# Three jobs of weight sums in the first pair of the second MLP instead of two, and another order of its SBUF pools

## The chip, the cores and the metric

One NeuronCore of a Trainium2 chip runs the whole program. The metric is the device time of one execution in microseconds; lower is better.

## The reference

Attention with sparse masks feeds two MLPs, all in float32:

```python
x = attention(q, k, v)            # 2304 tokens x 512; q, k, v: 4 x 8 heads x 576 x 64
h = np.maximum(x @ w_in, 0.0)     # w_in 512 x 2048
x = (s * h * h + b) @ w_out       # w_out 2048 x 512
a = x @ w_a                       # w_a, w_b 512 x 1536
b2 = x @ w_b
out = (a * b2) @ w_out2           # w_out2 1536 x 512
```

## The kernel before, in words

TensorE multiplies in float32r, each factor split into a high and a low part, three products for one. The first MLP runs in blocks of tokens (`n`), and in each over 16 columns of weights (`f`): `h_mm`, then `o_mm` two steps later. The last block is `n == NB - 1`. Its accumulators leave for `o1s` tiles, which are stored to DRAM for the second MLP.

The second MLP uses a Strassen-like form: every 2 by 2 block product needs seven products, and four sums of the weights' quarters (`s1` to `s4`). One call of the generator `sums(g, ...)` is one **job**: it loads two tiles `w2r` from DRAM on POOL's queue, makes the four sums in a tile `w2t` on DVE, copies highs on ACT into a room, subtracts lows on DVE, and stores the lot to DRAM on POOL's queue. Jobs 0 to 11 belong to w_a and w_b (two stores of 512 KB, `w2s`), jobs 12 to 17 to w_out2 (four stores, 1,792 KB together, `w2o`). A job of the second kind takes 14 steps of the generator: the loads, four sums, four copies, four subtractions, the stores and the end.

Sixteen jobs run in the last block of the first MLP, one called at each `f` by `work(f)`, in the order 0 to 3, 12 to 15, 4 to 11. Their highs lie, from the fourth job on, in one tile `room` of the pool `xp1` (`spare_s`, two places used in turn; `spare_a` beside it serves the jobs of w_out2 alone). Jobs 16 and 17 run in the first pair of the second MLP, spread over its groups one step at a time by `job_at` and `job_step`; their highs lie in buffers of the ring of g forms (`gf`).

The second MLP goes over three pairs of token blocks; in each, 12 groups `g` make seven products of six matmuls each (`a11`, `s2`, `s3`, `s1`, `a12`, `a22`, `s4`, in that order on TensorE) and gather them in `quad` tiles (one of pool `gq` for two groups); the last matmuls (`o2_mm`) follow. A group's weights come by `fill` and `source` on SP's queue: `wf` straight from `w2s`, and `wsrc`, which ACT and DVE split into `wf` and `wh`. Two helpers, `act` and `dve`, keep ACT's and DVE's instructions of this part in the order of the program.

In group 0 the first product is copied by ACT into the first quad (`u = qd[:, 1]`). The fifth product (`a12`) goes to the same PSUM bank, so it waits for that copy.

The pools that close with the first MLP (`mlp1.close()`) are, in KB of a partition: `xp0` 0 to 16, `xp1` 16 to 30, `wpb` 30 to 78 (counted from the first of them). The second MLP's pools lie over them in the order of their opening: `ws` 4, `tmp` 9, `rp` 15, `gq` 36, `rq` 12, `wx` 2, and each new tile waits for every use of each old tile that it lies over, as a whole (`reuse_waits="tile"`). So in the kernel before `gq` begins at 28 KB; its first tile, 28 to 34 KB, lies over the last 2 KB of `room`, where `spare_a` ends, and over `wpb`.

Of the kernel before, what the change touches and what calls it, by code (L numbers as in the profile page):

```python
# [27 lines left out]
def sparse_attention_two_mlps(  # L28
# [22 lines left out]
    NF1 = FF1 // P  # L51
# [52 lines left out]
    @contextmanager  # L104
    def after(instructions):
        with ExitStack() as st:
            for i in instructions:
                st.enter_context(tc.issue_after(i))
            yield

    def in_order(step, *args):
        with after(list(last_pe)):
            return step(*args)
# [7 lines left out]
    def split(hi, lo, src):  # L121
        nc.scalar.activation(out=hi, in_=src, func=AF.Copy)  # L122
        return nc.vector.tensor_tensor(out=lo, in0=src, in1=hi.bitcast(F32), op=ALU.subtract)
# [726 lines left out]
    p2 = None  # L850
    NG2 = NF2
    NQ2 = NF2 // 2
    EARLY = NF1

    def sums(g, room, vector, scalar):
        own = g < NG2
        first_ = 6 * (g // 2) + g % 2 if own else 6 * (g - NG2) + 2
        r = [p2.tile([P, DM], F32, tag="r", name="w2r", bufs=4) for _ in range(2)]
        for t, i in zip(r, (first_, first_ + 3)):
            nc.gpsimd.dma_start(out=t, in_=w2d[i])  # L860
        yield
        quarter = lambda t, i: t[:, i * HALF:(i + 1) * HALF]
        a11, a22 = quarter(r[0], 0), quarter(r[1], 1)
        a12, a21 = (quarter(r[0], 1), quarter(r[1], 0)) if own else (quarter(r[1], 0), quarter(r[0], 1))
        t = p2.tile([P, 4, HALF], F32, tag="s", name="w2t", bufs=2)
        s2, s1, s3, s4 = (t[:, i] for i in range(4))
        for out_, in0, in1, op in (
            (s1, a21, a22, ALU.add), (s2, s1, a11, ALU.subtract),
            (s3, a11, a21, ALU.subtract), (s4, a12, s2, ALU.subtract),
        ):  # L870
            vector(out=out_, in0=in0, in1=in1, op=op)  # L871
            yield
        flat = lambda t: t.rearrange("p i c -> p (i c)")
        zs, zh, zl = room(g)
        n = 4 * HALF // len(zs)
        halves_ = [(flat(t)[:, i * n:(i + 1) * n], z) for i, z in enumerate(zs)]
        lows = [i.bitcast(F32R) for i, _ in halves_]
        if not own:
            halves_ += [(r[1], zh[:, HALF:]), (a11, zh[:, 0:HALF])]
            lows += [zl[:, HALF:], zl[:, 0:HALF]]  # L880
        for src, high in halves_:
            scalar(out=high, in_=src, func=AF.Copy)  # L882
            yield
        for (src, high), low in zip(halves_, lows):
            vector(out=low, in0=src, in1=high.bitcast(F32), op=ALU.subtract)
            yield
        m = (2 if own else 4) // len(zs)
        for e in range(2):
            for i, z in enumerate((zs, lows)[e][:len(zs)]):
                nc.gpsimd.dma_start(  # L890
                    out=w2s[g][:, :, e] if own else w2o[g - NG2][:, 3 + i * m:3 + (i + 1) * m, e],
                    in_=z.bitcast(F32).rearrange("p (i c) -> p i c", i=m),
                )
            if not own:
                nc.gpsimd.dma_start(
                    out=w2o[g - NG2][:, 0:3, e], in_=(zh, zl)[e].bitcast(F32).rearrange("p (i c) -> p i c", i=3)
                )
        yield
# [36 lines left out]
    def x2_load(pair):  # L935
        xr = p2.tile([P, 2, KD, TB2], F32, tag="xr", name="xr")
        for i in range(2):
            c0 = (2 * pair + i) * TB2
            queue_sp(out=xr[:, i], in_=o1[:, c0:c0 + TB2].rearrange("(k p) t -> p k t", p=P))
        return xr  # L940
# [164 lines left out]
    for n in range(NB):  # L1105
        acc = [ps_acc.tile([P, TM], F32, tag="acc", name="acc") for _ in range(KD)]
        if n == 1:
            with after(list(behind)):
                split(bc[:, 0], bc[:, 1], b_sb.to_broadcast([P, 2]))
        if n + 1 == NB:  # L1110
            assert not steps
            att.close()
            p2 = ctx.enter_context(tc.tile_pool(name="p2", bufs=1, reuse_waits="tile", side="right"))
            spares = cycle(range(2))
            rooms_s = lambda g: (
                [spare if len(begun) < 4 else spare_s[next(spares)]], *(spare_a if g >= NG2 else 2 * [None])
            )
            first_jobs = [*range(0, 4), *range(NG2, NG2 + NQ2 - 2), *range(4, NG2)]
            added, begun = [sums(g, rooms_s, nc.vector.tensor_tensor, nc.scalar.activation) for g in first_jobs], []
            next(added[0])  # L1120
            spare = p2.tile([P, 2 * DM], F32R, tag="z", name="spare")
            xr = x2_load(0)
            ahead = [x2_bias(xr), x2_forms(xr)]

            def work(j):
                if j + 1 < EARLY:
                    next(added[j + 1])
                begun.append(j)
                for _ in added[j]:
                    pass  # L1130

        for f in range(NF1):
            order = ExitStack()
            if n == 0:
                supply(len(wi) + len(wo) + 6)
                with after(behind + (last_w if f == 1 else []) or last_act + last_dve):
                    next_weights(min(1 if f == 0 else 2, len(order1) - len(wi) - len(wo)))
                order.enter_context(after(last_act + last_dve))
            gt = in_order(h_mm, n, f)
            queue.append((acc, gt, f, n))  # L1140
            if len(queue) > AHEAD1:
                in_order(o_mm, *queue.pop(0))
            attend(n * NF1 + f)
            order.close()
            if n == NB - 1:
                last_act[:], last_dve[:] = list(behind), list(behind)
                for _ in range(4 if f < 2 else 0):
                    next(ahead[0])
                if f:
                    next(ahead[1], None)  # L1150
                with after(list(behind)):
                    if f == 3:
                        room = xp[1].tile([P, 7 * DM], F32R, tag="x", name="spare")
                        spare_a = [room[:, 4 * DM + i * 3 * HALF:4 * DM + (i + 1) * 3 * HALF] for i in range(2)]
                        spare_s = [room[:, 2 * DM * i:2 * DM * (i + 1)] for i in range(2)]
                    work(f)
                if f == 8:
                    wsrc = p2.tile([P, 3 * HALF], F32, tag="z", name="wsrc")
                    source("a11", 0)
                    source("a22", 0)  # L1160
                if f in (4, 8, 12):
                    next(ahead[1])
                if f == 10:
                    fill("s2", 0)
                if f == 11:
                    fill("a11", 0)
                    source("a11", 1)
                if f == 12:
                    fill("s3", 0)
                if f == 13:  # L1170
                    fill("a11", 1)
                    fill("s2", 1)
                if f == 14:
                    fill("s3", 1)
                if f == 15:
                    source("a11", 2)
            elif n:
                for st in later:
                    st(T1[n], f + 1 < NF1)
    for item in queue:  # L1180
# [1 line left out]

    mlp1.close()
    pool = lambda name, bufs: ctx.enter_context(tc.tile_pool(name=name, bufs=bufs, reuse_waits="tile"))
    ws, tmp, rp, gq, rq, wx = (
        pool(*i) for i in (("ws", 2), ("tmp", 6), ("rp", 5), ("gq", NQ2), ("rq", 4), ("wx", 1))
    )

    def add(out_, in0, in1, op=ALU.add):
# [129 lines left out]
    source("a22", 1)  # L1319
    ring_row = [rings[i].rearrange("p e c -> p (e c)") for i in (5, 11, 4, 10)]  # L1320
    rooms_s = lambda g: ([i[:, 0:DM] for i in ring_row[0:2]], *ring_row[2:])
    added = [sums(g, rooms_s, partial(dve, "tensor_tensor"), act) for g in range(NG2 + NQ2 - 2, NG2 + NQ2)]
    job_at = {}
    for j in range(2):
        g = 4 * j + 3
        for at in (
            (2 * j, 1), *((g, k) for k in (1, 2, 3, 4)), *((g + 1, k) for k in (4, 5, 6, 7)),
            *((g + 2, k) for k in (1, 2, 3, 4)), (g + 2, 5),
        ):
            job_at[at] = added[j]  # L1330

    def job_step(i, k):
        if (i, k) in job_at:
            in_order(next, job_at[i, k], None)

    sets = [[ps_acc.tile([P, TM], F32, tag="acc", name="o2")[:, 0:TB2] for _ in range(2)] for _ in range(2)]
    for pair in range(NP2):
        quads = []
        later_x = []
        for g in range(NG2):  # L1340
            i = pair * NG2 + g
# [134 lines left out]
```

## Time and profile before

| what | value |
|---|---|
| median of 3 runs | 917.77 us (916.84 to 919.07) |
| the profiled execution's own time | 917.58 us |
| its span, first to last instruction | 915.5 us |
| TensorE busy (matmul) | 880.0 us, 96% of the span |
| VectorE busy | 681.1 us, 74% |
| ScalarE busy | 406.8 us, 44% |
| GpSimd busy | 144.2 us, 16% |
| mean granted TensorE clock | 0.988 |

Times in views are microseconds from the span's start. TensorE is the engine that is nearly always busy; what the other engines do matters where TensorE waits for it.

### The profile page before, as it was taken

How to read it: one execution, taken by the hardware profiler on the slowest of the kernel's cores; microseconds unless marked ns; L12 is line 12 of the kernel's file. 1: busy time of each engine (PE TensorE's matmuls, PEld its weight loads, DVE VectorE, ACT ScalarE, POOL GpSimd, SP SyncE). 2: the span in 40 equal slices, each digit the busy share in tenths (PEclk: the TensorE clock that was granted, in tenths of full speed). 3: DMA queues.
4: the chain of work that ended last, by engine and by line, in shares of the span. 5: the costliest groups of instructions: out<-in, count | busy, mean ns of one | idle time of the engine just before them, and what ended most of it. 6: DMA issues, size and time to landing. Idle time of an engine off the chain costs nothing.

```text
span 915.5 us, 17296 instructions
## 1 busy us (share of the span) xinstructions
PE 880.0 (96%) x6274; PEld 806.0 (88%) x6274; DVE 681.1 (74%) x1411; ACT 406.8 (44%) x878; POOL 144.2 (16%) x288
## 2 busy tenths in 40 slices
PE   8999999999999999999994898999999999999997
PEld 6778889998888899978784898999999999999996
DVE  6898885776767677637765686898677797877793
ACT  6777764434333353366653232454233362322250
POOL 6000000000000010115534010104400005100013
PEclk9999999999999999999997899999999999999999
DMA  9966434666765676269999577689567589566586
GB/s 222 283 206 183 143 77 133 158 163 167 203 166 154 154 217 182 69 219 320 341 347 323 173 233 266 232 277 344 164 209 265 186 264 315 180 208 199 167 264 175
DMA packets 184612, 195.70 MB, mean 214 GB/s; under 512 B 108240, under 2 KB 137680, under 8 KB 184528
## 3 DMA queue, kind: packets, MB, share of 16 engines
q1 hardware_dynamic: 166160, 147.07, 54.2%
q0 software_dynamic: 15488, 46.81, 14.8%
q10 hardware_dynamic: 2880, 0.72, 0.5%
q8 instruction: 50, 0.82, 0.4%
q14 instruction: 34, 0.28, 0.1%
HBM read 152.08 MB, written 42.47 MB: 212 GB/s over the span
## 4 chain that ended last, share of the span: by engine, by line
PE 79%; DMA 8%; ACT 4%; DVE 3%; issue 3%; POOL 1%; SPq 0%; POOLq 0%; ACTq 0%; DVEq 0%
PE pp L99 26%; PE h L99 18%; PE acc L99 16%; PE o L99 13%; DMA w2s<-w2t 2%; DMA o2w<-w2o 2%; DMA wsrc<-w2d 2%; PE po L99 2%; PE pss L99 1%; PE ppt L102 1%; DVE w2t L871 1%; PE fpo L99 1%; DMA fqk<-in_q_dram 1%; POOL w2r L860 1%; ACT spare L882 1%
## 5 line engine op out<-in xcount | busy, mean ns | idle before, releaser
L99 PE MATMUL pp<-x2w,wf 128*128 128x384 f32 x1296 | 235.3, 338 | 18.2 <-ACT quad L613 14.4
L99 PEld LDWEIGHTS pp<-x2w,wf 128*128 128x128 f32 x1296 | 227.9, 190 | 20.1 <-ACT quad L613 14.8
L99 PE MATMUL h<-x,w 128*128 128x512 f32 (+1 forms) x960 | 217.5, 375 | 2.9 <-ACT r L795 2.9
L99 PE MATMUL acc<-gt,w 128*128 128x512 f32 (+2 forms) x960 | 211.0, 369 | 1.1 <-ACT w L122 1.0
L99 PEld LDWEIGHTS acc<-gt,w 128*128 128x128 f32 x960 | 175.5, 188 | 24.4 <-ACT w L122 1.4
L99 PEld LDWEIGHTS h<-x,w 128*128 128x128 f32 x960 | 171.6, 188 | 28.3 <-ACT r L795 4.3
L99 PE MATMUL o<-gf,o2w 128*128 128x384 f32 x756 | 134.0, 337 | 2.9 <-DMA o2w<-w2o 2.2
L99 PEld LDWEIGHTS o<-gf,o2w 128*128 128x128 f32 x756 | 131.1, 188 | 5.3 <-issue 4.0
L613 ACT ACTIVATE gf<-quad 128x384 fp32r<-128x384 f32 x126 | 64.1, 522 | 91.5 <-DVE quad L618 68.4
L795 ACT ACTIVATE r<-h 128x512 f32<-128x512 f32 (+1 forms) x80 | 44.3, 553 | 123.7 <-PE h L99 114.2
L1274 POOL DMA_DIRECT2D out_dram<-ot x92 | 51.5, 567 | 275.3 <-DVE ot L1260 269.7
L805 DVE TENSOR_TENSOR r<-r 128x384 f32<-128x384 f32 (+1 forms) x48 | 28.9, 603 | 59.6 <-ACT gt L802 59.5
L618 DVE TENSOR_TENSOR gf<-quad,gf 128x384 fp32r<-128x384 f32 x126 | 67.6, 555 | 7.1 <-ACT gf L613 5.2
L618 DVE TENSOR_TENSOR quad<-pp,quad 128x384 f32<-128x384 f32 x108 | 59.8, 554 | 17.1 <-DMA w2r<-w2d 8.3
L613 ACT ACTIVATE wf<-wsrc 128x512 fp32r<-128x512 f32 x36 | 22.6, 628 | 67.3 <-PE pp L99 51.1
L847 POOL DMA_DIRECT2D w2d<-w2s x36 | 19.7, 546 | 206.8 <-DVE w2s L157 191.4
L613 ACT ACTIVATE quad<-pp 128x384 f32<-128x384 f32 x36 | 17.6, 488 | 71.7 <-PE pp L99 62.7
L141 ACT ACTIVATE raw<-raw 128x512 f32<-128x512 f32 x66 | 42.6, 672 | 7.4 <-DMA raw<-in_moe_w_a_dram 6.3
L147 DVE SCALAR_TENSOR_TENSOR raw<-raw 128x512 uint32<-128x512 uint32 x66 | 44.4, 688 | 0.7
L99 PE MATMUL pp<-x2w,wh 128*128 128x384 f32 x216 | 44.2, 340 | 0.0
L618 DVE TENSOR_TENSOR wf<-wsrc,wf 128x512 fp32r<-128x512 f32 x36 | 24.9, 692 | 23.1 <-ACT wf L613 21.4
L618 DVE TENSOR_TENSOR quad<-quad 128x384 f32<-128x384 f32 x72 | 40.0, 555 | 1.3
(174 smaller groups left out, 1003.4 us busy)
## 6 DMA issues: line engine op xcount, KB each, us to landing
wf<-w2s SPq DMA_DIRECT2D x72, 512.0 KB
o2w<-w2o SPq DMA_DIRECT2D x126, 256.0 KB
raw<-in_moe_w_out_dram SPq DMA_DIRECT2D x28, 512.0 KB
w2d<-w2s POOLq DMA_DIRECT2D x36, 256.0 KB, 3.8
w2r<-w2d POOLq DMA_DIRECT2D x36, 256.0 KB, 4.6
wsrc<-w2d SPq DMA_DIRECT2D x36, 256.0 KB
raw<-in_moe_w_in_dram SPq DMA_DIRECT2D x16, 512.0 KB
raw<-in_moe_w_a_dram SPq DMA_DIRECT2D x12, 512.0 KB
```

The costliest lines, as they stand in the source:

```text
L99: last_pe[:] = [nc.tensor.matmul(*args, **kwargs).ins]
L102: last_pe[:] = [nc.tensor.transpose(*args).ins]
L141: nc.scalar.activation(out=high.bitcast(F32), in_=high.bitcast(F32), func=AF.Copy, scale=HIGH_SCALE)
L147: nc.vector.scalar_tensor_tensor(out=low, in0=high, scalar=3, in1=low, op0=ALU.logical_shift_left, op1=ALU.bitwise_or)
L613: i = nc.scalar.activation(**kwargs).ins
L618: i = getattr(nc.vector, method)(**kwargs).ins
L795: relu = nc.scalar.activation(out=r, in_=ph, func=AF.Relu)
L805: nc.vector.tensor_tensor(out=r, in0=r, in1=r, op=ALU.mult)
L847: nc.gpsimd.dma_start(out=w2d[i - 1], in_=w)
L860: nc.gpsimd.dma_start(out=t, in_=w2d[i])
L871: vector(out=out_, in0=in0, in1=in1, op=op)
L1274: engines[k % len(engines)].dma_start(out=at.rearrange("(j t) c -> t j c", t=STR), in_=st[i * STR:(i + 1) * STR, j:j + m].rearrange("t j a ...
```

## The change

The last block of the first MLP gets 15 jobs, one at each `f` but the last: 0 to 3, 12 to 14, 4 to 11. Job 15 goes to the first pair of the second MLP, which now has jobs 15, 16 and 17. Their steps are set out anew: (group, step) (0, 1) to (3, 5) for the first, (2, 1) to (5, 7) for the second; the third keeps the places that job 17 had. The stores of a job follow its last subtraction. The pool `wx` is opened before `gq`, so `wx` lies at 28 to 30 KB, `gq` at 30 to 66, `rq` at 66 to 78.

```diff
-    EARLY = NF1
+    EARLY = NF1 - 1
...
-            first_jobs = [*range(0, 4), *range(NG2, NG2 + NQ2 - 2), *range(4, NG2)]
+            first_jobs = [*range(0, 4), *range(NG2, NG2 + NQ2 - 3), *range(4, NG2)]
...
                 if j + 1 < EARLY:
                     next(added[j + 1])
                 begun.append(j)
-                for _ in added[j]:
-                    pass
+                if j < EARLY:
+                    for _ in added[j]:
+                        pass
...
-    ws, tmp, rp, gq, rq, wx = (
-        pool(*i) for i in (("ws", 2), ("tmp", 6), ("rp", 5), ("gq", NQ2), ("rq", 4), ("wx", 1))
+    ws, tmp, rp, wx, gq, rq = (
+        pool(*i) for i in (("ws", 2), ("tmp", 6), ("rp", 5), ("wx", 1), ("gq", NQ2), ("rq", 4))
     )
...
-    added = [sums(g, rooms_s, partial(dve, "tensor_tensor"), act) for g in range(NG2 + NQ2 - 2, NG2 + NQ2)]
+    added = [sums(g, rooms_s, partial(dve, "tensor_tensor"), act) for g in range(NG2 + NQ2 - 3, NG2 + NQ2)]
     job_at = {}
-    for j in range(2):
-        g = 4 * j + 3
-        for at in (
-            (2 * j, 1), *((g, k) for k in (1, 2, 3, 4)), *((g + 1, k) for k in (4, 5, 6, 7)),
-            *((g + 2, k) for k in (1, 2, 3, 4)), (g + 2, 5),
-        ):
-            job_at[at] = added[j]
+    for job, at in zip(added, (
+        ((0, 1), *((1, k) for k in (1, 2, 3, 4)), *((2, k) for k in (4, 5, 6, 7)), *((3, k) for k in (1, 2, 3, 4, 5))),
+        ((2, 1), (3, 5), (3, 6), (3, 7), (4, 7), *((5, k) for k in (1, 2, 3, 4))),
+        ((4, 1), *((7, k) for k in (1, 2, 3, 4)), *((8, k) for k in (4, 5, 6, 7)), *((9, k) for k in (1, 2, 3, 4, 5))),
+    )):
+        for i in at:
+            job_at.setdefault(i, []).append(job)
+    for k in (4, 5, 6, 7, 7):
+        job_at.setdefault((5, k), []).append(added[1])
 
     def job_step(i, k):
-        if (i, k) in job_at:
-            in_order(next, job_at[i, k], None)
+        for gen in job_at.get((i, k), ()):
+            in_order(next, gen, None)
```

## Rows read from the trace of the kernel before

**Rows 1.** Waits of PE in the whole run: us in total, times, longest.

```profile
PE pp L99 <- ACT quad L613: 14.4, 1, 14.4
...
PE pp L99 <- DVE quad L618: 2.5, 1, 2.5
...
PE pp L99 <- DMA wf<-w2s: 1.2, 1, 1.2
```

**Rows 2.** Timeline around the wait: start, us, engine, line, what, [idle before, releaser].

```profile
493.45 0.76 DVE L871 TENSOR_TENSOR w2t<-w2r 128x256 f32<-128x256 f32 x2 [1.10 <-DMA w2s<-w2t]
493.66 0.69 ACT L827 ACTIVATE o1s<-acc,sb 128x512 f32<-128x512 f32 x1 [2.57 <-DMA o<-o1s]
...
494.63 0.56 POOL L860 DMA_DIRECT2D w2r<-w2d  x1 [1.31 <-DMA o<-o1s]
...
496.92 0.68 POOL L890 DMA_DIRECT2D w2s<-spare  x1 [0.55 <-ACT spare L882]
498.18 0.69 POOL L890 DMA_DIRECT2D w2s<-w2t  x1 [0.58 <-DVE w2t L885]
...
505.64 0.49 ACT L613 ACTIVATE quad<-pp 128x384 f32<-128x384 f32 x1 [9.01 <-DMA w2s<-w2t]
```

**Rows 3.** Timeline of PE in the first pair's groups.

```profile
506.18 2.29 PE L99 MATMUL pp<-x2w,wf 128*128 128x384 f32 x6 [14.43 <-ACT quad L613]
508.27 2.12 PE L99 MATMUL pp<-x2w,wh 128*128 128x384 f32 x6
...
516.87 1.20 PE L99 MATMUL pp<-x2w,wh 128*128 128x384 f32 x6
...
524.15 1.20 PE L99 MATMUL pp<-x2w,wh 128*128 128x384 f32 x6
...
538.71 1.20 PE L99 MATMUL pp<-x2w,wh 128*128 128x384 f32 x6
...
553.27 1.21 PE L99 MATMUL pp<-x2w,wh 128*128 128x384 f32 x6
...
566.51 1.20 PE L99 MATMUL pp<-x2w,wh 128*128 128x384 f32 x6
...
573.79 1.20 PE L99 MATMUL pp<-x2w,wh 128*128 128x384 f32 x6
...
581.31 1.20 PE L99 MATMUL pp<-x2w,wh 128*128 128x384 f32 x6
```

**Rows 4.** Chain that ended last, the stretch 498 to 562: start, us, what.

```profile
498.18 7.37 DMA w2s<-w2t
...
548.71 11.05 DMA wsrc<-w2d
```

**Rows 5.** Windows: stretch, length, busy (instructions) of engines, granted clock, DMA share, GB/s.

```profile
487.40:506.18 18.78, 4.35 (x25) 4.03 (x23) 7.87 (x14) 3.99 (x5) 6.29 (x10) 0.68 0.95 335
...
506.18:510.30 4.12, 4.12 (x13) 4.12 (x14) 2.35 (x4) 1.31 (x3) 0.00 (x0) 0.50 0.04 13
510.30:517.90 7.60, 7.60 (x43) 7.60 (x42) 3.95 (x8) 1.43 (x3) 0.00 (x0) 0.95 0.47 147
...
525.20:532.50 7.30, 7.30 (x44) 7.30 (x44) 5.83 (x13) 1.90 (x5) 0.00 (x0) 1.00 0.64 204
532.50:539.75 7.25, 7.25 (x43) 7.25 (x42) 6.80 (x14) 2.17 (x5) 0.00 (x0) 1.00 0.59 193
...
554.36:567.55 13.19, 9.50 (x44) 8.89 (x44) 6.27 (x14) 3.68 (x9) 0.00 (x0) 0.87 0.65 236
```

**Rows 6.** Instructions of the tiles w2t and w2r: count, ns minimum/median/maximum, first and last start.

```profile
L618 DVE TENSOR_TENSOR w2t<-w2r x4: 415/417/419, 527.3 to 564.1; 128x256 f32<-128x256 f32 x4
...
L618 DVE TENSOR_TENSOR w2t<-w2t,gf x4: 681/684/684, 542.3 to 579.8; 128x512 fp32r<-128x512 f32 x4
...
L618 DVE TENSOR_TENSOR gf<-w2r,gf x4: 417/552/684, 544.7 to 581.9; 128x512 fp32r<-128x512 f32 x2, 128x256 fp32r<-128x256 f32 x2
```

**Rows 7.** DVE's timeline in group 4.

```profile
538.37 0.55 DVE L618 TENSOR_TENSOR quad<-pp,quad 128x384 f32<-128x384 f32 x1
```

## Prediction

> **What bounds the kernel now.** I read the page's busy shares first: TensorE is at 96% of the span, so a change gains only where TensorE stands still. The waits of TensorE come next [rows 1]. One line stands out: the products wait once for ACT's `quad`, 14.4 us; every other wait of the second MLP is under 3 us. So this one wait is what the change can be worth, and I ask what ended it.
>
> The timeline answers [rows 2]. TensorE starts group 0 at 487.40 and does four products, 4.35 us [rows 5]. The fifth adds into the bank of the first, so it needs ACT's copy of that bank into the first quad. ACT makes that copy at 505.64, after 9.01 us in which it was put down to a store of `w2t`. The chain of waits says the same: the store issued at 498.18 lands after 7.37 us, and then the copy goes [rows 4]. But the copy reads a PSUM bank and writes a quad; it has nothing to do with `w2t`, whose pool lies elsewhere. By the pools' addresses the first quad (28 to 34 KB) lies over the end of `room`, and `room`'s last use is the store of the highs, issued at 496.92 on the same queue just before [rows 2]. I take that store to be the releaser; the two land too close together for the row to tell them apart. The wait is false in this sense: the 2 KB that overlap belong to `spare_a`, which only the jobs of w_out2 use, and those are done long before. It is the rule of whole tiles that makes the copy wait for job 15's `spare_s`.
>
> The restart costs as well. After the wait the granted clock is 0.50, the lower level of 1.2 GHz, in 506.18 to 510.30, and 0.95 in the 7.6 us after it, against 1.00 later [rows 5]. In numbers: from 506.18 to the sixth product's start at 516.87 TensorE does 48 matmuls in 10.69 us; a whole group of 42 takes 524.15 - 516.87 = 7.28 us [rows 3], so 48 would take 8.32. The slow restart costs 2.37 us.
>
> Why is job 15 so late? In 487.40 to 506.18 the DMA engines are busy 0.95 of the time at 335 GB/s [rows 5], and DVE waits for a store of `w2t` before that job's first sum [rows 2]. The jobs run behind their places in the program because DMA carries no more.
>
> **The change part by part.**
>
> *The pools' order.* The first quad moves to 30 to 36 KB, over `wpb` alone, the weights of the first MLP. TensorE reads these last in its final `o_mm`, before the first product of group 0, so ACT's copy has nothing of them left to wait for. `wx` takes 28 to 30 KB and is used only at the pair's end. Gain: the wait of 14.43 us [rows 3] and the restart of 2.37, together 16.80 us. Not all need come: from below, zero, if something else holds the copy (rivals).
>
> *One job fewer in the block.* TensorE does not wait there to speak of, so nothing is gained in the block itself. The removed job is one of the large ones: 512 KB loaded and 1,792 KB stored, 2.36 MB, which at 335 GB/s is 7.0 us of the DMA engines. I estimate that the last stores land 7.0 us earlier, at about 505.55 - 7.0 = 498.5 (498.18 + 7.37 is 505.55, [rows 4]).
>
> *What is late next, groups 0 to 2.* Group 0 now runs on to 487.40 + 7.28 = 494.68 and group 2 starts near 502, where in the kernel before the pause let the DMA engines clear (share 0.04 after it, [rows 5]). Three things can be late. (a) ACT's copy stands behind the `o1s` evictions; one of these waited 2.57 us for a store of the one before, for want of a `w2r` buffer [rows 2]. With job 15's buffers free this should go; if it stays, the eviction ends near 491 and the copy near 491.5, just when it is needed at 491.75. (b) The first moved job loads at step (0, 1) and sums at (1, 1), about 495.7. Before, its like had until group 3. The load's POOL instruction waited for an `o1s` store until 494.63 [rows 2]; the evictions come some 4 us earlier now, so I put the load at 490.5 and its landing at 497 to 499. The chained order of DVE puts the next PSUM reads behind the sum, and TensorE needs the sum of `pd` at about 499.9 (five products after 494.68). It would fit barely or cost 1 to 2 us. (c) `wsrc` for the quarters of groups 1 and 2 goes out behind the `o1s` stores, into DMA engines that are full until 498.5. I take 1.5 us for the three; bounds 0 and 6.0 (a case like group 7's, below).
>
> *The third job in groups 1 to 3.* DVE gets four sums of 0.417 us (1.67) and subtractions of 3 x 0.684 + 0.417 = 2.47 us more [rows 6]; ACT, busy 2.17 of 7.25 us in such a group [rows 5], has room for four copies. In group 1 DVE is busy 3.95 of 7.60, so the sums lie beside other work. Group 3 had 5.83 [rows 5] with an old job's sums; it now has 5.83 - 1.67 + 2.47 + 3 x 0.417 = 7.88 us of a group's 7.28, and group 4 has 6.80 + 0.42 = 7.22. So DVE falls behind by some 0.6 to 1.25 us. In group 4 it ends its read of the fourth product's bank at 538.37 + 0.55 = 538.92 [rows 7], and the seventh product needs that bank one product, a seventh of 7.28 us, after 538.71 [rows 3], at 539.75, 0.83 us later: the loss is 0 to 0.4 us. The stores, 1.83 MB in groups 2 and 3 where DMA stands at 204 GB/s [rows 5], add 126 GB/s over two groups, 330 in all, about the 335 above. The nearest case is the last job's stores in group 9: 581.31 - 573.79 = 7.52 against 7.28, a loss of 0.24 us [rows 3]. I take 0.8 us for all of this part, bounds 0.2 and 2.
>
> On these stores the Trainium skill has a rule, on the page "DMA: Bandwidth & Descriptors", section "Queues, rings and completion order": each DMA engine takes turns between the queues that have work for it, packet by packet. A weight load on SP's queue would then get about half of each engine while POOL's stores last, and be late in group 2 or 3. The trace bears both out: 11.05 us for one `wsrc` load in group 5 to 7 [rows 4], against 0.24 us lost in group 9. By the rule at its worst the sum would end 5.2 us higher; I keep that as a rival.
>
> *The second job, groups 5 to 7.* The trace has a stall there already: from 553.27 to 566.51 is 13.24 us for one group, 5.96 over 7.28 [rows 3], of which 1.2 and 2.5 us are waits for `wf` and for DVE [rows 1] and the rest the clock (0.87 in that stretch, [rows 5]). Behind it is the load of the next pair's `xr`, 1.5 MB, that meets job 16's stores in group 5 and delays `wsrc` by 11.05 us [rows 4]. The change leaves `xr` where it is, and job 16's stores fall in the same groups, its subtractions four steps later. DVE's backlog hides under this stall, for TensorE waits for the load anyway; if that cover went, the 2.47 us of subtractions in group 5's second half would cost up to about 1.5. Stores that come later leave DMA idle first and full after. I take +0.5 us; bounds -3 (the load meets less) and +3.
>
> *The third job's places, groups 7 to 9,* are those of job 17: nothing.
>
> Sum: -16.80 + 1.5 + 0.8 + 0.5 = -14.0. From the profiled execution's 917.58 us that gives 903.6; the median of the runs shown is 0.19 us above it, so **903.8 us**.
>
> **Rivals.**
>
> *A. The wait moves to a transfer in groups 0 to 3.* The first moved job's load, or a `wsrc`, lands some 4 us later than I put it; DVE, in the program's order, stands still, and TensorE pays a wait and a slow restart as in group 7: 5.96 us instead of the 1.5 (or 0.8) taken. For it: DMA at 0.95 to the end of the block, and only 8 us from (0, 1) to (1, 1). Against it: 7.0 us of transfers are gone. Time 908.3, up to 911 when the load lands as late as the last store did before.
>
> *B. The change does not do what it says.* If the copy waits for `w2t`'s store after all, as the row has it, or something else tied to the last job, it goes at 498.5 instead of 505.55: 7.1 us gained and no clock, 917.8 - 7.1 + 0.8 + 0.5 = 912. For it: the releaser's name. Against it: the pool of `w2t` is no part of the quad's.
>
> *C. Slower: short waits hold the clock down.* With DVE behind from group 3 on, TensorE could wait a little at each product, and the granted clock fall to 0.50. At that level 12 matmuls took 4.12 us [rows 5] instead of 2.08, so a group costs 7.2 us more. The gain of 14.0 is spent from 1.9 groups at the lower level on; three groups give 903.8 + 21.5 = 925. For it: 0.87 around the stall of group 7. Against it: DVE at 6.80 of 7.25 us leaves the clock at 1.00 [rows 5], and only one group goes over 7.28.
>
> **How the numbers follow.** Forecast, 900.0 to 907.5 us: 0.71. Below 900, if no new cost comes and the block gains too: 0.03. A: 0.14, of which I count 0.10 below 910. B: 0.06. C: 0.04. No change that can be measured, which is within 0.2% or 1.8 us for this kernel: 0.02. The range 900 to 910 holds 0.81. Faster by over 0.2% are the first four cases, 0.94; same 0.02; slower 0.04.
>
> **What would show it.** Right: TensorE's wait for ACT's `quad` gone, no stretch at clock 0.50 after the block, `wh` products of groups 0 and 1 some 7.28 us apart, the last `w2s` store landing near 498.5. The stall at group 7 should still be there at about its size, the PE row of group 4 within 0.5 us of 7.28. Wrong: a wait of DVE for `w2r` or of ACT for `wsrc` above 3 us in groups 1 to 3 with TensorE behind it (A); a wait for `quad` that ends with a store (B); granted clock under 0.9 over several groups (C). The prediction fails most likely in groups 1 and 7, where I bound landing times of transfers by rows of another mix.

## The result and the profile after

905.11 us (median of 4 runs, 903.68 to 906.84) against 917.31 for the kernel before beside them: ratio 0.9868, 95% interval 0.9842 to 0.9894. The profiled execution took 903.68 us with a span of 902.0. The forecast was 903.8, or 903.6 for the profiled execution; the profiled one is the fastest of the four.

The waits of TensorE in the changed kernel (us in total, times, longest) no longer have the line with ACT's `quad` that led [rows 1]:

```profile
PE pp L99 <- DVE quad L618: 3.2, 5, 2.3
...
PE pp L99 <- DMA wf<-w2s: 1.0, 1, 1.0
PE pp L99 <- DVE c L618: 0.6, 1, 0.6
PE pp L99 <- DVE v L618: 0.6, 1, 0.6
```

ACT's timeline at the end of the block and in groups 0 to 2 (start, us, what, [idle before, releaser]):

```profile
486.41 0.69 ACT L827 ACTIVATE o1s<-acc,sb 128x512 f32<-128x512 f32 x1 [2.30 <-PE acc L99]
487.32 0.69 ACT L827 ACTIVATE o1s<-acc,sb 128x512 f32<-128x512 f32 x1 [0.22 <-PE acc L99]
488.18 1.06 ACT L882 ACTIVATE spare<-w2t 128x1024 fp32r<-128x1024 f32 x1 [0.17 <-DVE w2t L871]
489.14 0.47 ACT L613 ACTIVATE quad<-pp 128x384 f32<-128x384 f32 x1
...
504.01 0.63 ACT L613 ACTIVATE wf<-wsrc 128x512 fp32r<-128x512 f32 x1 [7.41 <-DMA wsrc<-w2d]
```

The copy into the first quad goes at 489.14, with no wait, where it went at 505.64 [rows 2]; TensorE needs it near 491.9. The evictions of `o1s` wait for TensorE alone. The next thing that is late stands in the last row: ACT waits 7.41 us for a `wsrc` in group 2. DVE and SP show what else is late, and the chain that ended last has that load's time:

```profile
499.08 0.42 DVE L618 TENSOR_TENSOR w2t<-w2r 128x256 f32<-128x256 f32 x1 [2.50 <-DMA w2r<-w2d]
...
504.68 0.69 DVE L618 TENSOR_TENSOR wf<-wsrc,wf 128x512 fp32r<-128x512 f32 x1 [2.30 <-ACT wf L613]
```

```profile
495.49 8.44 DMA wsrc<-w2d
...
536.12 11.04 DMA wsrc<-w2d
```

The moved job's first sum waits 2.50 us for its load; the `wsrc` issued at 495.49 takes 8.44 us to land, and one at 536.12, in front of group 7, 11.04 us as before [rows 4]. TensorE's rows, with the sixth product of each group (`wh`) as a mark [rows 3 have the like]:

```profile
492.80 1.20 PE L99 MATMUL pp<-x2w,wh 128*128 128x384 f32 x6
...
500.83 1.31 PE L99 MATMUL pp<-x2w,wh 128*128 128x384 f32 x6 [0.59 <-DVE v L618]
...
505.89 3.75 PE L99 MATMUL pp<-x2w,wf 128*128 128x384 f32 x18 [0.63 <-DVE c L618]
509.75 1.32 PE L99 MATMUL pp<-x2w,wh 128*128 128x384 f32 x6
...
517.65 1.20 PE L99 MATMUL pp<-x2w,wh 128*128 128x384 f32 x6
...
525.53 1.34 PE L99 MATMUL pp<-x2w,wh 128*128 128x384 f32 x6 [0.31 <-DVE quad L618]
...
533.40 1.20 PE L99 MATMUL pp<-x2w,wh 128*128 128x384 f32 x6
...
540.68 1.27 PE L99 MATMUL pp<-x2w,wh 128*128 128x384 f32 x6
...
549.12 4.96 PE L99 MATMUL pp<-x2w,wf 128*128 128x384 f32 x18 [2.32 <-DVE quad L618]
553.91 1.22 PE L99 MATMUL pp<-x2w,wh 128*128 128x384 f32 x6
```

What a group loses is the step from mark to mark less the 7.28 us of a group without waits. Group 1: 500.83 - 492.80 - 7.28 = 0.75; group 2: 8.92 - 7.28 = 1.64; groups 3, 4, 5: 0.62, 0.60, 0.59; group 6: 0.00; group 7: 13.23 - 7.28 = 5.95. Group 0 loses the time from the first product to its mark beyond five sevenths of 7.28. Over the twelve groups the kernel before lost 23.6 us and this one 10.5: that is 13.1 of the 13.9 us between the two profiled executions. (Each is a single execution; the medians differ by 12.2.)

For all kernels below, worked out in the same way from each one's TensorE timeline (us lost in groups; "rest" is groups 8 to 11):

```
kernel                      g0    g1    g2    g3    g4    g5    g6    g7   rest   sum
before                   15.67  1.32  0     0     0     0     0     5.96  0.64  23.59
changed                   0.03  0.75  1.64  0.62  0.60  0.59  0     5.95  0.30  10.48
changed, again            0.03  0.99  1.69  0.62  0.82  0.62  0     7.40  0.23  12.40
pools only                0.02  7.08  0.32  0.31  0     0     0     5.75  0.03  13.51
jobs only                 3.24  1.38  0     0     0     0.36  0     8.15  1.01  14.15
moved job left out        0.02  0     0.80  0.60  0     0     0     5.96  0.27   7.68
xr in group 4             0.03  0.78  1.35  0.61  0.67  0.62  1.32  0.62  0.26   6.26
loads by SP               0.02  0.49  0.13  0.20  1.21  0.60  0     7.22  0.58  10.46
second job later          0.03  0.68  1.13  0.60  0     1.28  0     2.75  0.19   6.66
second job later, again   0.02  1.11  1.56  0.61  0     0.32  0     3.35  0.41   7.38
later, xr in group 4      0.02  0.80  1.52  0.62  0     0.88  2.57  1.23  1.46   9.11
all three                 0.02  0     0     0.52  0.23  0.60  4.58  1.19  1.06   8.20
later, one load by SP     0.02  0     0.42  0.62  0     0.87  0     3.27  0.42   5.62
```

Each row is one execution. The two of the changed kernel differ by 1.9 us in sum and by 1.45 in group 7, the two with the second job later by 0.96 in group 5, so a difference of that size between two rows is not shown by them. The rows of "changed" and "later, one load by SP" come from the fastest execution of their kernel, those of "changed, again", "jobs only", "loads by SP", "later, xr in group 4" and "all three" from the slowest.

The block before it, from its first 512-column `h` matmul to group 0, took 95.1 to 98.6 us in these profiles, 95.07 before and 95.82 after, so single times of two kernels can differ by 3 us for a reason outside the groups. The long ones are the first four kernels below, measured side by side: 97.2 to 98.6 us, against 95.3 to 96.2 in the other profiles of changed kernels. In two of these, the moved job left out and `xr` in group 4, TensorE waits 1.97 and 1.98 us for ACT within the block and the next 12 matmuls take 4.6 us; in the changed kernel the same place costs 1.41 and 3.02:

```profile
439.30 4.60 PE L99 MATMUL h<-x,w 128*128 128x512 f32 x12 [1.97 <-ACT r L795]
```

```profile
437.99 3.02 PE L99 MATMUL h<-x,w 128*128 128x512 f32 x12 [1.41 <-ACT r L795]
```

### The profile page after: what moved, and what is told of

Read it like the earlier page. It is cut to its first block, busy times and chain, and to the rows that moved or that the text cites. A ratio compares the mean times of both kernels' runs of the same rounds, so it can differ in the third digit from the quotient of the medians.

```text
span 902.0 us, 17304 instructions
## 1 busy us (share of the span) xinstructions
PE 880.0 (98%) x6274; PEld 803.7 (89%) x6274; DVE 679.9 (75%) x1412; ACT 405.5 (45%) x879; POOL 145.8 (16%) x290
## 4 chain that ended last, share of the span: by engine, by line
PE 78%; DMA 7%; DVE 4%; ACT 4%; issue 3%; POOL 2%; SPq 0%; POOLq 0%; DVEq 0%; ACTq 0%
PE pp L99 25%; PE h L99 18%; PE acc L99 16%; PE o L99 13%; DMA wsrc<-w2d 3%; DMA w2s<-w2t 2%; PE po L99 2%; PE pss L99 1%; PE ppt L102 1%; DMA o2w<-w2o 1%; PE fpo L99 1%; DVE quad L618 1%; POOL w2r L860 1%; ACT fpt L613 1%; DMA xr<-o 1%
```

## Experiments

**The order of the pools alone.** The kernel before with

```diff
-    ws, tmp, rp, gq, rq, wx = (
+    ws, tmp, rp, wx, gq, rq = (
```

> The kernel before with the new order of the pools alone: 16 jobs stay in the block, two in the first pair. Theory (the wait was false: the first quad lay over the tile of the jobs' highs, whose last store had to land): TensorE's 14.4 us wait for ACT's quad is gone or under 2 us, since ACT's copy now stands before job 15's copy in ACT's order; the DMA engines stay full to about 505, so weights come late in groups 1 and 2 and cost 2 to 6 us; 904 to 909 us. Rival (the copy waited for the store of the sums' tile, as the row names it, or for anything else of job 15): the wait stays, 915 to 919 us.

(Here and in the prediction "job 15", and in the next expectation "job 14", is counted by place: it is the last job of the block, which by its number is job 11.)

910.27 us, ratio 0.9927 (0.9906 to 0.9948). ACT's and TensorE's timelines, the SP issue that they wait for, and POOL's last two stores:

```profile
490.37 0.49 ACT L613 ACTIVATE quad<-pp 128x384 f32<-128x384 f32 x1 [1.42 <-PE pp L99]
...
495.45 0.68 ACT L827 ACTIVATE o1s<-acc,sb 128x512 f32<-128x512 f32 x1
...
503.29 0.42 ACT L613 ACTIVATE wh<-wsrc 128x256 fp32r<-128x256 f32 x1 [3.74 <-DMA wsrc<-w2d]
```

```profile
504.68 4.21 PE L99 MATMUL pp<-x2w,wf 128*128 128x384 f32 x12 [4.98 <-DVE quad L618]
508.69 1.52 PE L99 MATMUL pp<-x2w,wh 128*128 128x384 f32 x6
```

```profile
498.10 0.58 SPq L119 DMA_DIRECT2D wsrc<-w2d  x1
```

```profile
501.61 0.72 POOL L890 DMA_DIRECT2D w2s<-spare  x1
...
502.75 0.85 POOL L890 DMA_DIRECT2D w2s<-w2t  x1
```

The copy waits for TensorE's product only and goes over 11 us before the last job's two stores are issued; all 16 jobs still run in the block. So neither store has to come before the copy: the wait was false, and it hung on the place of the first quad. Which of the two stores had ended it in the kernel before can be read from their landings (size, us from issue to landing):

```profile
w2s<-spare POOLq DMA_DIRECT2D x1, 512.0 KB, 8.5
w2s<-w2t POOLq DMA_DIRECT2D x1, 512.0 KB, 8.5
```

The store of the highs, issued at 496.92, landed near 505.4, and the copy went at 505.64. The store of `w2t`, issued at 498.18, landed near 506.7, when the copy had already begun: the row named the wrong one.

The rival's 915 to 919 did not come, but the time is a little above the theory's 904 to 909: ACT's second `o1s` eviction comes only at 495.45, SP's queue issues the next `wsrc` behind the `o1s` stores at 498.10, and ACT, DVE and TensorE wait for it: 4.98 us, with a slow restart 7.08 us lost in group 1. The late transfers that I took for 2 to 6 us cost 7.

**The move of the job alone.** The changed kernel with the old order:

```diff
-    ws, tmp, rp, wx, gq, rq = (
+    ws, tmp, rp, gq, rq, wx = (
```

> The changed kernel with the old order of the pools: 15 jobs in the block, three in the pair, the first quad still over the jobs' tile. Theory: the copy waits for job 14's store of highs, issued near 489.5 and landed at 494 to 498, so TensorE waits some 3 to 7 us in group 0 and restarts slowly (about 2.4 us more), part of the later loss in groups 1 and 2 hides behind it; 908 to 913 us. Rival 1 (moving the job is what gains, the pools' order nothing): 904 to 906 us as the changed kernel. Rival 2 (the job's removal alone frees nothing): 917 us.

909.89 us, ratio 0.9915 (0.9885 to 0.9944).

```profile
491.84 0.68 POOL L890 DMA_DIRECT2D w2s<-spare  x1 [3.59 <-ACT spare L882]
```

```profile
497.12 1.59 PE L99 MATMUL pp<-x2w,wf 128*128 128x384 f32 x6 [2.69 <-ACT quad L613]
```

```profile
496.57 0.49 ACT L613 ACTIVATE quad<-pp 128x384 f32<-128x384 f32 x1 [5.03 <-DMA w2r<-w2d]
```

POOL stores the last highs at 491.84, ACT's copy goes 4.73 us later, and TensorE waits 2.69 us for it, as the theory has it, if a little less than its 3 to 7. The row names the load of `w2r`, issued at 492.76, as the releaser, which the pools' addresses exclude. So do the landings:

```profile
w2s<-spare POOLq DMA_DIRECT2D x1, 512.0 KB, 4.6
w2r<-w2d POOLq DMA_DIRECT2D x1, 256.0 KB, 5.3
```

The highs landed near 496.4, just before the copy at 496.57, the load near 498.1, after it: again a transfer issued near the store. Each part alone leaves one wait: with the pools alone the late `wsrc`, with the job alone the copy. The two parts save 10.1 and 9.4 us of the groups' loss and together 13.1, not 19.5, for it is one stall that both shorten. In medians it is 7.7 and 8.1 us against the kernel before beside them (918.01), and 12.2 for both; the profile of this run, 913.81 us, is its slowest execution.

This run shows a second thing. The moved job is in groups 1 to 3 here as in the changed kernel, with the same work for DVE, and groups 2 to 4 lose nothing. DVE is busy 6.14 us in group 3 and, in group 4, nearly all the time (columns as in [rows 5]):

```profile
522.77:530.30 7.53, 7.45 (x43) 7.13 (x42) 7.35 (x16) 1.84 (x6) 0.75 (x2) 1.00 1.03 400
```

So DVE's added work in groups 3 and 4, forecast as 7.88 and 7.22 us, costs nothing by itself.

**The moved job left out.**

```diff
-        queue_sp(out=w.bitcast(F32), in_=w2o[fp][:, W_FORM[O2[n][2]]])
+        queue_sp(out=w.bitcast(F32), in_=w2o[2 if fp == 3 else fp][:, W_FORM[O2[n][2]]])
...
-    for job, at in zip(added, (
+    for job, at in list(zip(added, (
...
-    )):
+    )))[1:]:
```

> The changed kernel without the moved job: job 15 runs nowhere, and the last products read the sums of job 14 in their place, so one sixth of the second MLP's last sums is computed from the wrong weights. Theory (groups 1 to 5 of the changed kernel take 4.2 us more than 7.28 each because of the moved job): all but 0.5 us of that goes, 900.5 to 902 us. Rival (in groups 1 and 2 it is the full DMA engines after the block that make weights late, and the moved job costs only its 1.8 us in groups 3 to 5): groups 1 and 2 keep over 1.5 us of loss, 902.5 to 904 us. The stall in group 7 stays in both, 5 to 6 us.

904.52 us, ratio 0.9854 (0.9828 to 0.988), outside both forecasts; its profiled block was 97.78 us long against 95.82, which covers the gain. By groups: 1 to 5 lose 1.43 us where the changed kernel loses 4.20. So the moved job costs 2.8 us: all of groups 1, 4 and 5 and half of group 2. The other half stays, 0.80, with ACT waiting for `wsrc` still, and 0.60 in group 3.

```profile
505.45 0.63 ACT L613 ACTIVATE wf<-wsrc 128x512 fp32r<-128x512 f32 x1 [5.82 <-DMA wsrc<-w2d]
```

```profile
493.20 1.19 POOL L860 DMA_DIRECT2D w2r<-w2d  x2 [0.16 <-issue]
494.38 0.72 POOL L890 DMA_DIRECT2D w2s<-w2t  x1
494.96 1.23 POOL L860 DMA_DIRECT2D w2r<-w2d  x2
```

These are the transfers of the block's end, as the rival has it, but not the block's stores alone. With job 15 out, POOL's queue runs ahead to the loads of jobs 16 and 17 and issues four loads of `w2r` here, as many as the changed kernel does. So this run leaves out the moved job's work and stores, and not the early loads; the loads are tested further below. Neither forecast was right alone.

**xr a group earlier.**

```diff
-            if pair + 1 < NP2 and g == 5:
+            if pair + 1 < NP2 and g == 4:
```

> The changed kernel with the next pair's tokens (xr, 1.5 MB) loaded in group 4 instead of group 5. Theory (the stall in group 7, 5.95 us, comes of xr meeting the second job's stores in front of a wsrc load): xr lands before those stores begin, the stall falls under 2 us, 900 to 902.5 us. Rival (the stores and wf loads alone make wsrc late there): the stall stays at 4 us or more, 904 to 906 us. Third way: xr now meets the first job's last stores and delays a wsrc one group earlier, a stall of like size moves to group 6, 904 to 907 us.

902.8 us, ratio 0.9836 (0.9811 to 0.9861), 0.3 above the theory's range; the block was the longest of all, 98.6 us. Group 7 loses 0.62 instead of 5.95, group 6 now 1.32. So the stall of group 7 needs `xr` where it was, in front of a `wsrc`; a smaller stall in group 6 is what came of the third way.

**Where the second and third job's loads are issued.**

```diff
-            nc.gpsimd.dma_start(out=t, in_=w2d[i])
+            (queue_sp if g > NG2 + NQ2 - 3 else nc.gpsimd.dma_start)(out=t, in_=w2d[i])
```

> The changed kernel with the loads of the second and third job in the pair issued on SP's queue, in their place of the program, instead of on POOL's, which runs ahead and issues the second job's at 494 to 495.4. Theory (the loss of 2.4 us in groups 1 and 2 is of full DMA engines, and the 1.8 us in groups 3 to 5 is DVE's backlog that starts there): 0.5 MB leaves the full stretch, 1.5 us at 335 GB/s, so wsrc in group 2 lands 1 to 2 us earlier; group 2 loses under 0.6 us and groups 3 to 5 together under 1.0; 902 to 904 us. Rival (the moved job's DVE work itself costs in groups 3 to 5, and group 2 waits for the block's stores): groups 1 to 5 keep over 3.5 us, 904.5 to 906 us.

905.25 us, ratio 0.9865 (0.9832 to 0.9899): no better. The first part of the theory held, groups 1 to 3 lose 0.82 instead of 3.01; the second did not, groups 3 to 5 lose 2.01 where under 1.0 was forecast. The second job's loads now go out at 506.6 and the third's at 522.5, in front of weights on the same queue, and ACT waits again:

```profile
518.84 0.63 ACT L613 ACTIVATE wf<-wsrc 128x512 fp32r<-128x512 f32 x1 [4.77 <-DMA wsrc<-w2d]
```

Group 4 loses 1.21 and group 7 7.22. What was saved early is not seen in the time. That the moved loads cost it later is not shown: the changed kernel's own executions lose 0.60 and 0.82 in group 4, 5.95 and 7.40 in group 7.

**The second job later.** Sums in group 4, copies in 5, subtractions and stores in 6:

```diff
-        ((2, 1), (3, 5), (3, 6), (3, 7), (4, 7), *((5, k) for k in (1, 2, 3, 4))),
+        ((2, 1), *((4, k) for k in (4, 5, 6, 7)), *((5, k) for k in (4, 5, 6, 7)), *((6, k) for k in (1, 2, 3, 4, 5))),
...
-    for k in (4, 5, 6, 7, 7):
-        job_at.setdefault((5, k), []).append(added[1])
```

> The changed kernel with the second job's steps set later: sums in group 4, copies in group 5, subtractions and stores in group 6. Theory (DVE has no time to spare in groups 3 to 5, so a backlog stays): groups 3 to 5 lose under 0.8 us instead of 1.8; the stores leave group 5, so xr meets them later and the stall of group 7 shrinks to 3 to 5 us, or moves; 902 to 904.5 us. Rival (the backlog comes of the late wsrc in group 2 alone): groups 3 to 5 keep over 1.4 us, 904.5 to 906 us.

901.06 us, ratio 0.9825 (0.9792 to 0.9859), better than forecast. Group 4 loses nothing, 5 more (1.28), so that groups 3 to 5 still lose 1.88 in this run: the part of the theory on DVE's backlog is not borne out in sum (in the repeat below they lose 0.93). The gain is in group 7, 2.75 instead of 5.95: the second job's six stores are issued from 530.53 to 543.61, around the loads of `xr` at 530.77, where the changed kernel has them from 530.75 to 538.53 behind `xr` at 529.91.

**Both, and all three.** The edits of the runs before, put together.

> The second job later as in the run before, and xr loaded in group 4. If the stall of group 7 is xr against stores, xr has the time from group 4 to group 6 alone: groups 6 and 7 lose under 1 us together (1.9 with xr in group 4 alone), groups 1 to 11 lose 4 to 5.5 us in all against 10.5 in the changed kernel; 899 to 902 us. Rival (weight loads alone fill DMA in these groups): groups 5 to 7 keep over 2 us, 902 to 904 us.

> All three: loads of the second and third job on SP's queue, the second job later, xr in group 4. If the three causes add, groups 1 to 11 lose 2 to 3.5 us in all; 898 to 901 us. Rival: SP's queue, which holds back every load behind one that waits for a buffer, delays weights by as much as it saves; no better than the run before, 900 to 903 us.

904.28 us (0.9859, 0.9826 to 0.9892) and 904.68 us (0.9856, 0.9817 to 0.9896). Both forecasts were wrong, and both times are above the rivals' too; what the rivals say came: with `xr` in group 4 and the second job later, groups 6 and 7 lose 3.8 us, and with the loads on SP's queue as well, 5.8, no better than the run before. TensorE waits for DVE there, DVE had waited for ACT before, and ACT for a `wsrc`; in the first of these, ACT waits longest at

```profile
537.42 0.63 ACT L613 ACTIVATE wf<-wsrc 128x512 fp32r<-128x512 f32 x1 [6.09 <-DMA wsrc<-w2d]
```

The cures don't add. I take it that each moves 1 to 2 MB to where another has just moved some, but which transfer holds back that `wsrc` I did not take apart.

**The best place, beside the changed kernel.** The second job later, with its loads alone on SP's queue:

```diff
-            nc.gpsimd.dma_start(out=t, in_=w2d[i])
+            (queue_sp if g == NG2 + NQ2 - 2 else nc.gpsimd.dma_start)(out=t, in_=w2d[i])
```

> The changed kernel once more, beside the next two on the same chip: 904 to 907 us; its group 7 loses 5 to 6 us again and groups 1 to 5 some 3.5 to 4.5 us.

> The version with the second job later, once more: if its gain over the changed kernel is real, 900.5 to 903 us, 3 to 5 us below the changed kernel in the same rounds, with under 4 us lost in group 7. If the difference was that of chips and executions, within 1.8 us of it.

> The second job later, and its loads alone on SP's queue. If the losses of groups 1 to 3 and of group 7 have separate causes, groups 1 to 3 lose under 1 us (2.4 with the second job later alone) and group 7 stays under 3.5: 899 to 901.5 us. If what DMA saves early comes back later, as with the loads of both jobs on SP's queue, group 7 grows by as much: 901 to 903 us.

905.81 us (ratio 0.9874, 0.9855 to 0.9893), 902.77 (0.9839, 0.9821 to 0.9858) and 900.73 (0.9824, 0.98 to 0.9847), measured side by side. The changed kernel lost more than expected, 7.40 us in group 7 and 4.74 in groups 1 to 5. The gain of the later job is real, 3.0 us, no execution of one kernel reaching into the other's. With the one load moved it is 5.1 us over the changed kernel, inside the forecast, with 1.04 us lost in groups 1 to 3 where under 1 was expected. The 2.0 us of that load alone are less sure, for one of its four executions, 903.78, is slower than all with the later job only. TensorE's timeline of that version:

```profile
493.56 1.20 PE L99 MATMUL pp<-x2w,wh 128*128 128x384 f32 x6
...
500.84 1.20 PE L99 MATMUL pp<-x2w,wh 128*128 128x384 f32 x6
...
508.54 1.31 PE L99 MATMUL pp<-x2w,wh 128*128 128x384 f32 x6
...
541.01 3.42 PE L99 MATMUL pp<-x2w,wf 128*128 128x384 f32 x18 [0.66 <-DVE quad L618]
546.46 3.39 PE L99 MATMUL pp<-x2w,wf 128*128 128x384 f32 x18 [2.04 <-DVE quad L618]
```

Groups 1 and 2 lose 0.0 and 0.42 us where the later job alone lost 1.11 and 1.56 beside it, and group 7 stays at 3.27 against 3.35. Here the two causes were separate: the loss of groups 1 and 2 comes with the load that POOL's queue ran ahead to.

## Why the prediction was right, point by point

*The wait and its releaser.* Right, and shown: with the pools' order alone the copy no longer waits for any store, though the last job's two are issued over 11 us after it. The prediction held that the trace can't tell the two stores apart; their landings do, 505.4 and 506.7 about a copy at 505.64. Rival B, in which the copy waits for something else of the last job, is out. What the prediction calls job 15 here is the sixteenth and last job, job 11; job 15 itself is the eighth.

*The gain of 16.80 us.* Groups 0 and 1 of the kernel before lost 15.67 + 1.32 = 16.99 us, which came back whole. The prediction gave it to the pools' order; the runs show that this needs both parts. The pools alone save 10.1 us in the groups, because the sixteen jobs and their transfers still stand in front of group 1's weights. I costed "one job fewer in the block" at nothing for TensorE in the block, which no run contradicts, and saw its 7.0 us of transfers; that the pools' gain hangs on them I did not say.

*The last stores.* Expected to land near 498.5, 7.0 us before 505.55. That is when the copy was let go; the last store landed near 506.7. In the changed kernel:

```profile
489.53 0.67 POOL L890 DMA_DIRECT2D w2s<-spare  x1 [3.00 <-ACT spare L882]
492.33 1.19 POOL L860 DMA_DIRECT2D w2r<-w2d  x2 [2.13 <-DMA o<-o1s]
493.51 0.72 POOL L890 DMA_DIRECT2D w2s<-w2t  x1
```

The last store took 7.3 us and landed near 500.8, 5.9 us earlier than before. The store of the highs went 7.4 us earlier than the 496.92 of before; that of `w2t` only 4.7, behind the moved job's two loads, which had waited 2.13 us. Whether the 7.4 us come of fewer bytes, as the prediction reckons, is not shown: with job 15 gone, each of jobs 4 to 11 is also called one `f` earlier.

*Groups 0 to 2.* 1.5 us taken, 0.03 + 0.75 + 1.64 = 2.42 measured, inside the bounds. (a) cost nothing. (b) was right in place and nearly in time: the sum goes at 499.08, with the load put at 497 to 499. (c) was the larger, a `wsrc` of 8.44 us, and it cost in group 2. What filled the DMA engines there was not the block's stores alone, as the prediction has it, but also the second job's loads, which POOL's queue issued early: in the two runs that move them and leave `xr`, group 2 loses 0.13 and 0.42.

*The third job in groups 1 to 3, 0.8 us.* The size was off, and so was the mechanism. Groups 3 to 5 lost 1.81 us. I put it down to DVE's 7.88 us in group 3; the trace has 6.91 of 7.89 there and 6.89 of 7.81 in group 4. The runs say otherwise: with the job moved alone, DVE had the same work and groups 2 to 4 lost nothing; with the job left out, groups 2 and 3 still lost 1.4 and then the loss ended. So it takes both, and I read it so: a late load in group 2 puts DVE behind, and the moved job's share is that DVE, fuller, doesn't catch up before group 6. That chain is argued. The nearest run to a test is the one with the loads on SP's queue: group 2 loses 0.13 there and group 3 0.20, but group 4 has a late `wsrc` of its own and loses 1.21. The stall that would follow from the Trainium skill's rule of turns (page "DMA: Bandwidth & Descriptors", section "Queues, rings and completion order") at this job's own stores did not come: in groups 3 and 4, where these stores run, ACT's waits name no transfer.

*Groups 5 to 7, +0.5 us.* Measured in group 7 -0.01 in the profile of the first result, +1.44 in the other (group 5's 0.59 is counted above). That the stall would stay, and that `xr` meeting stores makes it, was right: moving either one cut it, to 0.62 and to 2.75.

*The sum.* -16.99 + 2.42 + 1.81 + 0 is -12.8, with -0.3 in the last groups, -13.1 in the groups; the forecast had -14.0. The profiled executions differ by 13.9, the medians by 12.2. The costs were taken 1.4 us too low and the gain 0.2. That the profiled execution, 903.68 us, meets the forecast of 903.6 is luck: it is the fastest of four, and the second profile of the same kernel, 907.02 us, loses 12.4 us in its groups instead of 10.5.

*Rivals A and C.* A's mechanism was there, a late `wsrc` in group 2 and a late job's load in group 1, at less than half of its price, since the waits of TensorE stayed at 0.6 us and the clock did not fall. C did not come: the granted clock is 1.00 in groups 0 to 6 of the changed kernel. (Its price by the prediction's own rows is 7.1 us for a group, 3.5 times 4.12 - 2.08, and not 7.2.)

```profile
501.98:510.80 8.82, 8.04 (x43) 7.01 (x42) 6.41 (x14) 1.74 (x5) 0.00 (x0) 1.00 0.76 242
...
518.69:526.50 7.81, 7.50 (x42) 7.01 (x42) 6.89 (x17) 1.96 (x4) 1.19 (x2) 1.00 1.03 402
...
541.70:554.98 13.28, 9.78 (x45) 8.92 (x44) 6.60 (x15) 4.13 (x9) 0.00 (x0) 0.87 0.70 262
```

(Windows of the changed kernel, columns as in [rows 5]; the last is group 7.)

Open: why the block is longer in the first four kernels, which transfer stalls group 6 when `xr` and the second job are both moved, and how much of the job's move is bytes and how much its place.

## What to carry to other kernels

When a wait's releaser makes no sense for the data, look at the addresses and at the landing times: in this kernel a tile placed over another waits for all of its uses, and the fix is to place it over something long done. Then ask which transfers stand behind the stall that goes, for they are late next, and taking bytes out of that stretch may be half of the gain. An engine without spare time can keep a delay for several groups, so a late load in one group may be paid in three. Look also at what a queue runs ahead to: a load issued early can take bandwidth from those that are needed now. Here groups 1 and 2 lost 2.67 us with one job's load issued early and 0.42 with it in its place. That load and the same job's steps, moved together, gained 5.1 us; three moves at once gained under 2.

## What the runs showed of the hardware

The releaser that the profile names can be a neighbour of the true one: a store of `w2t` before, and a load of `w2r` in the run with the job alone, for the same copy into the same tile. Both landed 1 us or more after the copy had begun (506.7 against 505.64, 498.1 against 496.57), and the store of the highs 0.2 us before it, both times. The restart after a wait differs much from wait to wait: after 4.98 us (pools alone) the granted clock was 0.50 for the next 4.01 us, after 0.98 and 2.32 us close together (group 7 of the changed kernel) it was 0.87 over the group. After 1.29 and 2.51 us (its second profile) it was 0.51 for the next 5.75, 7.40 us lost, and after 0.66 and 2.04 us (the last version) it stayed at 1.00 over 539.15 to 549.70, so that a stall a little shorter cost 3.3 us instead of 5.95.
